# The second-layer matmuls of the last batch put in another order: two runs of narrow matmuls in a quad where there were five

## The chip, the cores and the metric

The kernel runs on 1 core of one Trainium2 chip. The metric is the time of one execution on the device, in microseconds (us), as the median of several runs. The core has five engines that run their own instruction streams: TensorE (PE) multiplies matrices, and its weight loads are shown apart (PEld); VectorE (DVE) and ScalarE (ACT) do elementwise work; GpSimd (POOL) here mostly starts one kind of DMA; SyncE (SP) starts the other DMAs. Each engine takes its instructions in the order in which the program lists them, and waits on semaphores for the others.

## The reference, cut to what matters

```python
# B, N, C = 4, 6080, 256; d_ff = 2048
qn = q / (norm(q, axis=1) + 1e-06); kn = k / (norm(k, axis=1) + 1e-06)
s = kn.transpose(0, 2, 1) @ qn / tau        # C x C for each batch
a = softmax(s, axis=-1)
x = (v @ a).reshape(B * N, C)
h = x @ w_in                                # C -> d_ff
g = h - tanh(h)
out = g @ w_out                             # d_ff -> C
```

Every token's 256 features are mixed by the batch's attention matrix, widened to 2048, passed through h - tanh(h) and brought back to 256.

## The kernel before, in words

**First layer.** For each batch the attention matrix is folded into `w_in` once, so that h is one product of v with a folded factor. The tokens of a batch are cut into 6 pairs of two blocks of up to 512 columns (the odd pair is 512 + 448), and d_ff into 8 slices; a `Quad` (L1138 on) is one pair with one slice: 2 x 2 blocks of 128 factor columns by 512 tokens. It is computed with 7 block products instead of 8 (p1 to p7, `product`, L1329), and each block product is three matmuls, because both operands are kept as an upper and a lower piece (L327, `products`: upper by lower, upper by upper, lower by upper). The sums stand in banks called x, y and z, and ScalarE copies x out (L1173) before the next product is added to it.

**The elements between.** Each of the four blocks 11, 12, 21 and 22 of a quad is made by a DVE addition (L1183), a tanh on ScalarE (L1300, L1195, L1207) and a subtraction; then ScalarE rounds it to its upper piece (`gh`, L1311) and DVE takes the lower piece (`gl`, L1315). In the last batch the subtraction of some blocks (11 and 12) is done by an adding DMA that POOL starts (`join`, L1198 and L1303): the tanh is negated and the DMA adds the block to it.

**Second layer.** Plain blocks (L1470, `second`) take 6 matmuls of 512 columns each: three into each of the two output halves m = 0 and m = 1. They are called ps_o. In pairs 1 to 5 of the last batch ("halved" pairs, 40 quads) the first column of the quad, blocks 11 and 21, is again computed with 7 products instead of 8, at half the width: 21 narrow matmuls of 256 columns (L1393, `second_halves`, ps_h), three for each product. Their inputs come as four items: b1 (one product), b2, t1 and t2 (two products each), made by `split` (L1216) from the tiles n, b and ts. The second column, items 22 and 12, stays plain: 12 matmuls of 512 columns. So a halved quad has 21 matmuls of the first layer and 12 + 21 of the second.

**What sets the order.** The program adds operations to a `Plan` in the order in which TensorE is to run them. Items that are ready for the second layer are appended to a list, `stream`; between the block products of the first layer the table `HALVES` says how much of it `drain` takes (a wide matmul counts 1, a narrow one 0.5; 22.5 for a quad), and `lag` is how far the second layer is held behind. The other engines' operations are then sorted by the plan by when TensorE needs them. So the order of `stream` sets where narrow and wide matmuls stand, and the plan moves ACT's and DVE's work after it. At the very end `stream.sort` puts the plain items of the last `LAST` quads behind everything else.

**A pair's ends.** The last quad of a pair completes the output; the two halves m = 0 and 1 of a column are copied out by DVE and ScalarE (L1493) and stored (L1496), and the first quad of the next pair writes the same banks again. For a halved pair the seven sums ps_h are joined by `gather_halves`: two ScalarE copies (L1417), then DVE additions (L1422, L1435 to L1437) and two stores (L1425).

Of the kernel before, what the change touches and what calls it, by code (L numbers as in the profile page):

```python
# [43 lines left out]
]  # L44
HALVES = [("p6",[]),("p2",[5.5,"c"]),("p5",[]),("p7",[5.0]),("p4",["d",2.5]),("p3",["a",4]),("p1",["b",5.5])]
HALF = NMAX // 2
LAST = 2
SHARE = 1
JOINED = [(),(11,12)]
PARTS = [(1,"start"),(2,"start"),(3,"start"),(4,"start")]  # L50
LATE = {(1,12):3.5,(2,11):2,(2,12):1.5}
SUMS_AT = 32
ENTER = 10
EARLY = 6
# [194 lines left out]
def act_cost(n):  # L249
    return 0.09 + n * 0.00084  # L250
# [15 lines left out]
def attn_moe(ctx: ExitStack, tc: tile.TileContext, qk, v4, qkT, tau, w_in, w_out, outT):  # L266
# [7 lines left out]
    B, N, _, C = qk.shape  # L274
# [853 lines left out]
    def halved(b, p):  # L1128

        return b == B - 1 and p > 0  # L1130
# [7 lines left out]
    class Quad:  # L1138
# [77 lines left out]
        def split(self, name, n, source, reads, place):  # L1216

            x = self.g[name] = {}
            if place is None:
                h, l = Buf(ring["gh"]), Buf(ring["gl"])  # L1220
            else:
                h = Buf(ring[place])
                l = Buf(f"{name}_{self.name}", h)

            def hi():
                if place is None:
                    x[0] = sb(g_p, "gh", [P, NMAX], F32R, f"gh{name}_{self.name}")[:, 0:n]
                else:
                    y = sb(qk_p, place, [P, GJ, 2, C], F32R, f"{name}_{self.name}").rearrange("p a x c -> p a (x c)")
                    x[0], x[1] = y[:, 0, 0:n], y[:, 1, 0:n]  # L1230
                nc.scalar.copy(x[0], source())

            def lo():
                if place is None:
                    x[1] = sb(g_p, "gl", [P, NMAX], F32R, f"gl{name}_{self.name}")[:, 0:n]
                nc.vector.tensor_sub(x[1], source(), x[0].bitcast(F32))

            plan.add("ACT", act_cost(n), hi, reads=reads, writes=[h])
            plan.add("DVE", dve_cost(n), lo, reads=[*reads, h], writes=[l])
            self.bufs["g", name] = h, l  # L1240
            stream.append((self, name))

        def sums(self, i):

# [44 lines left out]
        def finish(self, i, c):  # L1289

            if halved(self.b, self.p) and i % 10 == 1:
                return self.first_column(i)
            n, name = self.ns[i % 10 - 1], f"{i}_{self.name}"
            apart = self.joined(i)
            t, h, l = Buf(ring["t"]), Buf(ring["gh"]), Buf(ring["gl"])
            self.bufs["g", i] = h, l

            def tanh():
                self.tiles["t", i] = sb(g_p, "t", [P, NMAX], F32, f"t{name}")[:, 0:n]
                nc.scalar.activation(self.tiles["t", i], self.tiles[c][:, 0:n], AF.Tanh, scale=-1.0 if apart else 1.0)  # L1300

            def join():
                nc.gpsimd.dma_start(self.tiles["t", i], self.tiles[c][:, 0:n], accum_op=ALU.add)  # L1303

            def sub():
                x = self.tiles["t", i]
                nc.vector.tensor_sub(x, self.tiles[c][:, 0:n], x)  # L1307

            def hi():
                self.g[i] = [sb(g_p, "gh", [P, NMAX], F32R, f"gh{name}")[:, 0:n]]  # L1310
                nc.scalar.copy(self.g[i][0], self.tiles["t", i])  # L1311

            def lo():
                self.g[i].append(sb(g_p, "gl", [P, NMAX], F32R, f"gl{name}")[:, 0:n])
                nc.vector.tensor_sub(self.g[i][1], self.tiles["t", i], self.g[i][0].bitcast(F32))  # L1315

            plan.add("ACT", act_cost(n), tanh, reads=[self.bufs[c]], writes=[t])
            if apart:
                plan.add("POOL", 1.0, join, reads=[self.bufs[c]], writes=[t], port=False, lag=plan.JOIN_LAG + LATE.get((self.s, i), 0.0))
            else:  # L1320
                plan.add("DVE", dve_cost(n), sub, reads=[self.bufs[c]], writes=[t], port=not isinstance(c, str))
            plan.add("ACT", act_cost(n), hi, reads=[t], writes=[h])
            plan.add("DVE", dve_cost(n), lo, reads=[t, h], writes=[l])
            stream.append((self, i))

        def joined(self, i):
            return self.b == B - 1 and i in JOINED[halved(self.b, self.p)]
# [31 lines left out]
        return x.rearrange("p i n -> p (i n)")  # L1359

    stream = []
    outs = {}
    obufs = {}

# [79 lines left out]
    def second(quad, i):  # L1444

        if isinstance(i, str):
            yield from second_halves(quad, i)
            return
        b, p, s = quad.b, quad.p, quad.s
        row, c = i // 10 - 1, i % 10 - 1  # L1450
        n = quad.ns[c]
        f = 2 * s + row
        gh, gl = quad.bufs["g", i]
        key = b, p, c
        first = key not in obufs
        if first:
            obufs[key] = [0] + [Buf(3 + 2 * c + m) for m in range(KC)]
        done = obufs[key]
        done[0] += 1
        last = done[0] == 2 * NS2  # L1460

        parts = (0, 1, 0, 0), (0, 0, 0, 1), (1, 1, 0, 0), (1, 0, 0, 1), (1, 0, 1, 2), (0, 0, 1, 2)
        end = last and b == B - 1 and p == NP - 1
        if end:
            parts = parts[0:2] + parts[5:6] + parts[2:5]
        for m, part, x, j in parts:
            def run(m=m, part=part, x=x, j=j):
                if first and j == 0:
                    outs[key + (m,)] = bank(3 + 2 * c + m, f"ps_o_{b}_{p}_{c}_{m}")
                nc.tensor.matmul(  # L1470
                    outs[key + (m,)][:, 0:n], (wo_l if part else wo_h)[:, f, m * P:(m + 1) * P], quad.g[i][x],
                    start=first and j == 0, stop=last and j == 2, skip_group_check=True,
                )

            plan.add("PE", pe_cost(n), run, reads=[gl if x else gh, wobuf[s]], writes=[done[1 + m]])
            yield 1
        if last:
            at_ = b * N + pairs_of[b][p][0] + c * quad.ns[0]
            for m in range(KC):
                halves = b == B - 1  # L1480
                ob = Buf(ring[("t" if halves else "raw") if c else "ob"])
                tiles = {}

                def copy(m=m, tiles=tiles):
                    if halves:
                        tag = "t" if c else "ob"
                        tiles[0] = sb(g_p, tag, [P, NMAX], F32, f"ob_{b}_{p}_{c}_{m}")[:, 0:n]
                    elif c:
                        raw = sb(qk_p, "raw", [P, GJ, 2, C], F32, f"ob_{b}_{p}_{c}_{m}")
                        tiles[0] = raw[:, 0].rearrange("p x c -> p (x c)")[:, 0:n]  # L1490
                    else:
                        tiles[0] = sb(g_p, "ob", [P, NMAX], F32, f"ob_{b}_{p}_{c}_{m}")[:, 0:n]
                    (nc.scalar.copy if m else nc.vector.tensor_copy)(tiles[0], outs[key + (m,)][:, 0:n])  # L1493

                def store(m=m, tiles=tiles):
                    nc.sync.dma_start(outT[m * P:(m + 1) * P, at_:at_ + n], tiles[0])  # L1496

                plan.add("ACT" if m else "DVE", act_cost(n) if m else dve_cost(n), copy, reads=[done[1 + m]], writes=[ob])
                plan.add("SP", 0.35, store, reads=[ob], size=0.26, due=plan.pe_time + 8.0)
# [277 lines left out]
    for b in range(1, B):  # L1777
        g0 = (b - 1) * SLOTS
        first = NS2
# [13 lines left out]
    lag = LAG  # L1793
# [19 lines left out]
    for gs in range(TOTAL):  # L1813
        quad = quads.pop(gs)
        for what in beside.get((gs, "start"), ()):
            what()
        before, uneven = uneven, quad.ns[0] != quad.ns[1]
        if halves_from - 4 <= gs < halves_from:
            lag += 3
        if gs == halves_from:  # L1820
            lag += 3
        if before and not uneven:
            lag += ENTER if gs < halves_from else 0
            stream[-2:] = reversed(stream[-2:])
        for name, then in UNEVEN if uneven else HALVES if halved(quad.b, quad.p) else ORDER:
            if uneven and not before and name in ("p2", "p5"):
                drain(ENTER // 2)
            if name == "p1":
                if gs + 1 < TOTAL:
                    quads[gs + 1] = Quad(gs + 1)  # L1830
                    quads[gs + 1].product("p1")
            else:
                quad.product(name)
            for x in then:
                if not isinstance(x, str):
                    held = min(lag, x * SHARE if gs >= halves_from else x)
                    lag, x = lag - held, x - held
                    drain(x)
                else:
                    for what in beside.get((gs, x), ()):  # L1840
                        what()
# [66 lines left out]
```

## Time and profile before

| what | value |
|---|---|
| median of 3 runs | 2142.55 us (2141.93 to 2142.94) |
| the profiled execution: its own time | 2142.2 us |
| the profiled execution: its span, first to last instruction | 2140.4 us |
| PE busy | 2134.6 us (100%), 10026 matmuls |
| DVE busy | 1879.3 us (88%) |
| ACT busy | 1613.0 us (75%) |
| POOL busy | 106.8 us (5%) |
| DMA | 419.74 MB, mean 196 GB/s |

The span lies 1.8 us below the execution's own time; the rest is before the first and after the last instruction. The page names TensorE as the engine of 99% of the chain that ended last. Matmuls overlap in the pipeline: the length of one in a timeline (0.39 us for 512 columns) is longer than the distance to the next one's start, so in what follows matmuls are priced by the distance from start to start.

### The profile page before, as it was taken

The page shows a single profiled execution, that of the slowest core. Times are in us where ns is not written, and L with a number is a line of the kernel's source. Part 1 is how long each engine was busy: PE and PEld are TensorE (multiplying, and loading weights), DVE is VectorE, ACT ScalarE, POOL GpSimd, SP SyncE. Part 2 cuts the span into 40 slices and gives each one's busy share as a digit, 9 for nine tenths or more (in the row PEclk, how much of TensorE's full clock was granted, in tenths as well). Part 3 has the DMA queues.
Part 4 walks back from the last instruction along what each step waited for, and adds up shares of the span by engine and source line. Part 5 has one row for each costly group of instructions (what it writes and reads, how often), then busy time and mean ns, then how long its engine had stood idle before and what let it go on. Part 6 is the DMA issues. An engine that isn't in the chain of part 4 may idle for free.

```text
span 2140.4 us, 29514 instructions
## 1 busy us (share of the span) xinstructions
PE 2134.6 (100%) x10026; PEld 1802.5 (84%) x10026; DVE 1879.3 (88%) x3332; ACT 1613.0 (75%) x3015; POOL 106.8 (5%) x117
## 2 busy tenths in 40 slices
PE   9999999999999999999999999999999999999999
PEld 8888888888888888888888888888888888888888
DVE  8998988899898888888899888888888989899897
ACT  6677878777777787886777788887676777777776
POOL 5100000000000000000000000000000011111111
PEclk9999999999999999999999999999999999999999
DMA  9845675366335576643543567564353467887875
GB/s 388 302 163 196 213 252 215 137 202 214 136 136 190 212 244 212 217 163 108 199 138 126 180 231 242 200 224 161 110 198 121 157 200 212 232 222 212 232 210 138
DMA packets 145625, 419.74 MB, mean 196 GB/s; under 512 B 20866, under 2 KB 63106, under 8 KB 142914
## 3 DMA queue, kind: packets, MB, share of 16 engines
q1 hardware_dynamic: 133954, 396.87, 53.3%
q0 software_dynamic: 11520, 20.98, 5.4%
q8 instruction: 79, 1.29, 0.2%
q14 instruction: 72, 0.59, 0.1%
HBM read 329.19 MB, written 66.85 MB: 185 GB/s over the span
## 4 chain that ended last, share of the span: by engine, by line
PE 99%; DMA 1%; issue 0%; ACT 0%; SPq 0%; POOL 0%; POOLq 0%
PE ps_o L1470 43%; PE x L327 25%; PE y L327 12%; PE z L327 7%; PE ps_h L1393 5%; PE ps_s L327 3%; PE ps_s L654 2%; PE ps_s L652 1%; PE ps_w L327 1%; DMA t<-c 0%; DMA vhl<-qk_dram 0%; ACT ob L1493 0%; ACT gh L1311 0%; POOL n L1198 0%; SPq L594 0%
## 5 line engine op out<-in xcount | busy, mean ns | idle before, releaser
L327 PE MATMUL x<-v,f 128*128 128x512 f32 (+1 forms) x2304 | 628.3, 389 | 0.0
L1470 PE MATMUL ps_o<-gh,wo_l 128*128 128x512 f32 (+1 forms) x1376 | 533.4, 388 | 0.2 <-ACT ob L1493 0.2
L1470 PE MATMUL ps_o<-gh,wo_h 128*128 128x512 f32 (+1 forms) x1376 | 533.3, 388 | 0.0
L327 PEld LDWEIGHTS x<-v,f 128*128 128x128 f32 x2304 | 430.1, 188 | 84.5
L1315 DVE TENSOR_TENSOR gl<-t,gh 128x512 fp32r<-128x512 f32 (+1 forms) x688 | 456.7, 681 | 27.0 <-ACT gh L1311 26.0
L1311 ACT CAST gh<-t 128x512 fp32r<-128x512 f32 (+1 forms) x688 | 411.3, 616 | 35.3 <-DVE t L1307 20.5
L1470 PE MATMUL ps_o<-gl,wo_h 128*128 128x512 f32 (+1 forms) x1376 | 421.3, 387 | 0.0
L1300 ACT ACTIVATE t<-c 128x512 f32<-128x512 f32 x536 | 333.2, 624 | 89.0 <-DVE c L1183 82.8
L1307 DVE TENSOR_TENSOR t<-c,t 128x512 f32<-128x512 f32 (+1 forms) x496 | 334.9, 679 | 25.3 <-ACT t L1300 20.2
L1173 ACT COPY u<-x 128x512 f32<-128x512 f32 (+1 forms) x384 | 222.2, 579 | 166.9 <-PE x L327 164.0
L1183 DVE TENSOR_TENSOR c<-u,y 128x512 f32<-128x512 f32 (+1 forms) x384 | 259.3, 675 | 84.6 <-ACT u L1173 55.9
L327 PE MATMUL y<-v,f 128*128 128x512 f32 (+1 forms) x1152 | 320.4, 386 | 0.1
L1470 PEld LDWEIGHTS ps_o<-gl,wo_h 128*128 128x128 f32 x1376 | 258.4, 188 | 51.3
L1470 PEld LDWEIGHTS ps_o<-gh,wo_l 128*128 128x128 f32 x1376 | 258.4, 188 | 48.0 <-ACT ob L1493 0.6
L1470 PEld LDWEIGHTS ps_o<-gh,wo_h 128*128 128x128 f32 x1376 | 258.6, 188 | 47.5
L327 PEld LDWEIGHTS y<-v,f 128*128 128x128 f32 x1152 | 209.8, 188 | 36.6 <-DVE c L1183 0.5
L1183 DVE TENSOR_TENSOR c<-p,z 128x512 f32<-128x512 f32 x192 | 131.8, 686 | 36.1 <-PE z L327 33.4
L327 PE MATMUL z<-v,f 128*128 128x512 f32 x576 | 162.1, 390 | 0.0
L1300 ACT ACTIVATE t<-x 128x512 f32<-128x512 f32 x152 | 91.1, 599 | 93.2 <-PE x L327 92.5
L1307 DVE TENSOR_TENSOR t<-x,t 128x512 f32<-128x512 f32 x152 | 105.1, 691 | 44.2 <-ACT t L1300 43.5
L327 PEld LDWEIGHTS z<-v,f 128*128 128x128 f32 x576 | 108.1, 188 | 23.1
L1173 ACT COPY p<-x 128x512 f32<-128x512 f32 x192 | 112.9, 588 | 19.0 <-PE x L327 16.0
(215 smaller groups left out, 2193.8 us busy)
## 6 DMA issues: line engine op xcount, KB each, us to landing
f<-f_d SPq DMA_DIRECT2D x160, 896.0 KB, 4.6
raw<-qk_dram SPq DMA_DIRECT2D x104, 384.0 KB, 5.0
nt<-qkT_dram SPq DMA_DIRECT2D x96, 380.0 KB, 5.0
f_d<-f SPq DMA_DIRECT2D x32, 896.0 KB, 3.9
outT_dram<-ob SPq DMA_DIRECT2D x88, 256.0 KB, 3.2
vraw<-v_dram SPq DMA_DIRECT2D x20, 1024.0 KB, 7.8
sl<-so_d SPq DMA_DIRECT2D x40, 512.0 KB, 4.0
wt<-wt_d SPq DMA_DIRECT2D x24, 512.0 KB, 6.8
```

Source lines behind the costliest of these rows:

```text
L327: ins = nc.tensor.matmul(out, w, x, start=first and i == 0, stop=last and i == len(seq) - 1, skip_group_check=True,)
L652: nc.tensor.matmul(self.ps[:, 0:C], x[:, 1, k], x[:, 0, q], start=False, stop=last, skip_group_check=True)
L654: nc.tensor.matmul(self.ps.rearrange("p (a c) -> p a c", a=2), x[:, 0, k], x[:, :, q], start=first, stop=False, skip_group_check=True,)
L1173: nc.scalar.copy(self.tiles[to], self.tiles["X"][:, 0:n])
L1183: nc.vector.tensor_add(self.tiles[i], self.tiles[u], self.tiles[ps][:, 0:n])
L1300: nc.scalar.activation(self.tiles["t", i], self.tiles[c][:, 0:n], AF.Tanh, scale=-1.0 if apart else 1.0)
L1307: nc.vector.tensor_sub(x, self.tiles[c][:, 0:n], x)
L1311: nc.scalar.copy(self.g[i][0], self.tiles["t", i])
L1315: nc.vector.tensor_sub(self.g[i][1], self.tiles["t", i], self.g[i][0].bitcast(F32))
L1393: nc.tensor.matmul(outs[b, p, place][:, at_ * HALF:(at_ + 1) * HALF], weights(a, part), quad.g[name][x][:, half * HALF:(half + 1) * HALF], ...
L1470: nc.tensor.matmul(outs[key + (m,)][:, 0:n], (wo_l if part else wo_h)[:, f, m * P:(m + 1) * P], quad.g[i][x], start=first and j == 0, stop ...
```

## The change

The items of a halved quad no longer enter `stream` as they are made. A new function `enter` holds them until their turn in `SEQ`: 22, b1, b2, t1, t2, 12. `lag` grows by 2 and not by 3 where the halved pairs begin. `LAST` is 1: only the last quad's plain items stand behind everything else. In the first and the last quad of every pair of the last batch the six matmuls of a plain item run as three for output half 0 and then three for half 1; before, that was so for the very last item alone.

```diff
@@ -44,11 +44,12 @@
 ]
 HALVES = [("p6",[]),("p2",[5.5,"c"]),("p5",[]),("p7",[5.0]),("p4",["d",2.5]),("p3",["a",4]),("p1",["b",5.5])]
 HALF = NMAX // 2
-LAST = 2
+LAST = 1
 SHARE = 1
 JOINED = [(),(11,12)]
 PARTS = [(1,"start"),(2,"start"),(3,"start"),(4,"start")]
 LATE = {(1,12):3.5,(2,11):2,(2,12):1.5}
+SEQ = [22,"b1","b2","t1","t2",12]
 SUMS_AT = 32
 ENTER = 10
 EARLY = 6
@@ -1238,7 +1239,7 @@
             plan.add("ACT", act_cost(n), hi, reads=reads, writes=[h])
             plan.add("DVE", dve_cost(n), lo, reads=[*reads, h], writes=[l])
             self.bufs["g", name] = h, l
-            stream.append((self, name))
+            enter(self, name)
 
         def sums(self, i):
 
@@ -1321,7 +1322,7 @@
                 plan.add("DVE", dve_cost(n), sub, reads=[self.bufs[c]], writes=[t], port=not isinstance(c, str))
             plan.add("ACT", act_cost(n), hi, reads=[t], writes=[h])
             plan.add("DVE", dve_cost(n), lo, reads=[t, h], writes=[l])
-            stream.append((self, i))
+            enter(self, i)
 
         def joined(self, i):
             return self.b == B - 1 and i in JOINED[halved(self.b, self.p)]
@@ -1359,6 +1360,17 @@
         return x.rearrange("p i n -> p (i n)")
 
     stream = []
+    waiting = {}
+
+    def enter(quad, name):
+        if not halved(quad.b, quad.p):
+            stream.append((quad, name))
+            return
+        there, order = waiting.setdefault(quad.gs, (set(), list(SEQ)))
+        there.add(name)
+        while order and order[0] in there:
+            stream.append((quad, order.pop(0)))
+
     outs = {}
     obufs = {}
 
@@ -1461,7 +1473,7 @@
 
         parts = (0, 1, 0, 0), (0, 0, 0, 1), (1, 1, 0, 0), (1, 0, 0, 1), (1, 0, 1, 2), (0, 0, 1, 2)
         end = last and b == B - 1 and p == NP - 1
-        if end:
+        if end or b == B - 1 and (first or last):
             parts = parts[0:2] + parts[5:6] + parts[2:5]
         for m, part, x, j in parts:
             def run(m=m, part=part, x=x, j=j):
@@ -1818,7 +1830,7 @@
         if halves_from - 4 <= gs < halves_from:
             lag += 3
         if gs == halves_from:
-            lag += 3
+            lag += 2
         if before and not uneven:
             lag += ENTER if gs < halves_from else 0
             stream[-2:] = reversed(stream[-2:])
```

TensorE, steady state, from the narrow matmuls of quad 1 on to quad 2, pair 2 of the last batch. A name ends in batch, pair, quad, sometimes a bank or half, and a serial number: x, y, z are first-layer sums, gh12 and gl12 the pieces of item 12, glb1 and ghb1 those of b1. Before:

```order
L1393 MATMUL ps_h_3_2_7_19131<-t2_3_2_1_19160,wo_h_95 128x256
L1393 MATMUL ps_h_3_2_7_19131<-t2_3_2_1_19160,wo_l_96 128x256
L1470 MATMUL ps_o_3_2_1_0_19057<-gh12_3_2_1_19205,wo_l_96 128x512
L1470 MATMUL ps_o_3_2_1_0_19057<-gh12_3_2_1_19205,wo_h_95 128x512
L1470 MATMUL ps_o_3_2_1_1_19063<-gh12_3_2_1_19205,wo_l_96 128x512
L1470 MATMUL ps_o_3_2_1_1_19063<-gh12_3_2_1_19205,wo_h_95 128x512
L327 MATMUL x_3_2_3_19190<-v5_3_2_18652,f_163_18964 128x512 x3
L1470 MATMUL ps_o_3_2_1_1_19063<-gl12_3_2_1_19215,wo_h_95 128x512
L1470 MATMUL ps_o_3_2_1_0_19057<-gl12_3_2_1_19215,wo_h_95 128x512
L1393 MATMUL ps_h_3_2_3_19043<-glb1_3_2_2_19241,wo_h_95 128x256
L327 MATMUL y_3_2_3_19246<-v6_3_2_18514,f_163_18964 128x512 x3
L1393 MATMUL ps_h_3_2_3_19043<-ghb1_3_2_2_19228,wo_h_95 128x256
```

Now, from the same product of quad 3 on:

```order
L328 MATMUL x_3_2_3_19189<-v5_3_2_18733,f_163_18966 128x512 x3
L1482 MATMUL ps_o_3_2_1_0_19037<-gl12_3_2_1_19236,wo_h_95 128x512
L1482 MATMUL ps_o_3_2_1_0_19037<-gh22_3_2_2_19205,wo_l_96 128x512
L1482 MATMUL ps_o_3_2_1_0_19037<-gh22_3_2_2_19205,wo_h_95 128x512
L328 MATMUL y_3_2_3_19243<-v6_3_2_18517,f_163_18966 128x512 x3
L1482 MATMUL ps_o_3_2_1_1_19054<-gh22_3_2_2_19205,wo_l_96 128x512
L1482 MATMUL ps_o_3_2_1_1_19054<-gh22_3_2_2_19205,wo_h_95 128x512
L1482 MATMUL ps_o_3_2_1_1_19054<-gl22_3_2_2_19215,wo_h_95 128x512
L1482 MATMUL ps_o_3_2_1_0_19037<-gl22_3_2_2_19215,wo_h_95 128x512
L328 MATMUL x_3_2_4_19302<-v0_3_2_18163,f_164_19095 128x512 x3
L1405 MATMUL ps_h_3_2_3_19070<-glb1_3_2_2_19263,wo_h_95 128x256
L1405 MATMUL ps_h_3_2_3_19070<-ghb1_3_2_2_19252,wo_h_95 128x256
```

The narrow matmuls of t2 and b1, which stood as a run of 2, a run of 1 and a run of 2 between wide ones, have left this place; t2 now ends the run of 11 ahead of it, and b1 heads a run of 10 behind it. The run of 5 grew to 10, and the run of 11 is as long as before.

ScalarE, quad 4 of pair 2 (u3 is the copy of x that the next product waits for, n11 the tanh that a POOL DMA joins). Before:

```order
L1195 ACTIVATE n11_3_2_4_19372<-c11_3_2_4_19348 128x512
L1173 COPY u3_3_2_4_19378<-x_3_2_4_19303 128x512
L1231 CAST t1_3_2_3_19383<-ts_3_2_3_19363 128x512
L1231 CAST t2_3_2_3_19391<-ts_3_2_3_19363 128x512
L1207 ACTIVATE t21_3_2_4_19396<-x_3_2_4_19303 128x512
```

Now:

```order
L1174 COPY u3_3_2_4_19376<-x_3_2_4_19302 128x512
L1232 CAST t1_3_2_3_19381<-ts_3_2_3_19365 128x512
L1232 CAST t2_3_2_3_19389<-ts_3_2_3_19365 128x512
L1208 ACTIVATE t21_3_2_4_19394<-x_3_2_4_19302 128x512
L1196 ACTIVATE n11_3_2_4_19401<-c11_3_2_4_19345 128x512
```

The tanh of block 11 has moved from ahead of u3 to behind the tanh of block 21, four operations later.

TensorE, the last two quads of the program. Before:

```order
L1393 MATMUL ps_h_3_5_7_21988<-t2_3_5_6_22561,wo_h_95 128x256 x2
L1393 MATMUL ps_h_3_5_7_21988<-t2_3_5_6_22561,wo_l_96 128x256
L1393 MATMUL ps_h_3_5_3_21903<-glb1_3_5_7_22629,wo_h_95 128x256
L1393 MATMUL ps_h_3_5_3_21903<-ghb1_3_5_7_22616,wo_h_95 128x256
L1393 MATMUL ps_h_3_5_3_21903<-ghb1_3_5_7_22616,wo_l_96 128x256
L1393 MATMUL ps_h_3_5_3_21903<-b2_3_5_7_22603,wo_h_95 128x256 x2
```

Now:

```order
L1405 MATMUL ps_h_3_5_7_21980<-t2_3_5_6_22578,wo_h_95 128x256 x2
L1405 MATMUL ps_h_3_5_7_21980<-t2_3_5_6_22578,wo_l_96 128x256
L1482 MATMUL ps_o_3_5_1_0_21893<-gh12_3_5_6_22582,wo_l_96 128x512
L1482 MATMUL ps_o_3_5_1_0_21893<-gh12_3_5_6_22582,wo_h_95 128x512
L1482 MATMUL ps_o_3_5_1_1_21912<-gh12_3_5_6_22582,wo_l_96 128x512
L1482 MATMUL ps_o_3_5_1_1_21912<-gh12_3_5_6_22582,wo_h_95 128x512
L1482 MATMUL ps_o_3_5_1_1_21912<-gl12_3_5_6_22592,wo_h_95 128x512
L1482 MATMUL ps_o_3_5_1_0_21893<-gl12_3_5_6_22592,wo_h_95 128x512
L1405 MATMUL ps_h_3_5_3_21927<-glb1_3_5_7_22640,wo_h_95 128x256
L1405 MATMUL ps_h_3_5_3_21927<-ghb1_3_5_7_22632,wo_h_95 128x256
L1405 MATMUL ps_h_3_5_3_21927<-ghb1_3_5_7_22632,wo_l_96 128x256
```

Quad 6's item 12, six wide matmuls, moved from behind the last narrow run to ahead of it. On DVE the order behind the last narrow run is as before: five additions of L1422 and L1435 to L1437, then gl12 of quad 7, two more additions, and the copy of output half 0; only ahead of them have gl22 and the last lower piece of t2 changed places.

## Rows read from the trace of the kernel before

**Rows 1.** Cores and page, part 1: span and granted clock; busy time of TensorE.

```profile
core 0: 2140.4 us, clock 1.000
PE 2134.6 (100%) x10026; PEld 1802.5 (84%) x10026; DVE 1879.3 (88%) x3332; ACT 1613.0 (75%) x3015; POOL 106.8 (5%) x117
```

**Rows 2.** Waits of TensorE, whole span: engine line waited for, us, times, longest.

```profile
PE idle L1851 <- DVE ones L319: 1.1, 1, 1.1
PE ps_s L327 <- DMA vhl<-qk_dram: 0.4, 1, 0.4
PE ps_o L1470 <- ACT ob L1493: 0.2, 1, 0.2
```

**Rows 3.** TensorE timeline, 512-column stretch: start, length, engine, line, operation, count.

```profile
1550.25 0.84 PE L327 MATMUL x<-v,f 128*128 128x512 f32 x3
...
1555.91 0.39 PE L1470 MATMUL ps_o<-gh,wo_h 128*128 128x512 f32 x1
```

**Rows 4.** TensorE timeline, one quad of the last batch.

```profile
1840.66 0.28 PE L1393 MATMUL ps_h<-t,wo_h 128*128 128x256 f32 x1
...
1840.89 0.40 PE L1470 MATMUL ps_o<-gh,wo_l 128*128 128x512 f32 x1
...
1842.96 0.28 PE L1393 MATMUL ps_h<-glb,wo_h 128*128 128x256 f32 x1
1843.07 0.86 PE L327 MATMUL y<-v,f 128*128 128x512 f32 x3
1843.77 0.28 PE L1393 MATMUL ps_h<-ghb,wo_h 128*128 128x256 f32 x1
...
1844.00 0.40 PE L1470 MATMUL ps_o<-gh,wo_l 128*128 128x512 f32 x1
...
1846.05 0.40 PE L1393 MATMUL ps_h<-b,wo_h 128*128 128x256 f32 x2
...
1846.64 0.86 PE L327 MATMUL x<-v,f 128*128 128x512 f32 x3
...
1848.03 0.28 PE L1393 MATMUL ps_h<-b,sl 128*128 128x256 f32 x1
...
1849.34 0.86 PE L327 MATMUL y<-v,f 128*128 128x512 f32 x3
...
1850.73 0.28 PE L1393 MATMUL ps_h<-t,wo_h 128*128 128x256 f32 x1
```

**Rows 5.** TensorE timeline, where the last batch passes to its second pair.

```profile
1727.82 0.39 PE L1470 MATMUL ps_o<-gh,wo_l 128*128 128x512 f32 x1
1728.35 0.96 PE L327 MATMUL y<-v,f 128*128 128x512 f32 x3
```

**Rows 6.** Timeline of all engines, the last microseconds.

```profile
2131.71 0.41 DVE L1422 TENSOR_TENSOR ob<-s,ps_h 128x256 f32<-128x256 f32 x1
...
2133.55 0.68 DVE L1315 TENSOR_TENSOR gl<-t,gh 128x512 fp32r<-128x512 f32 x1
...
2134.60 0.81 SPq L1425 DMA_DIRECT2D outT_dram<-ob  x2
...
2135.34 0.39 PE L1470 MATMUL ps_o<-gl,wo_h 128*128 128x512 f32 x1
...
2136.45 0.59 ACT L1493 COPY ob<-ps_o 128x512 f32<-128x512 f32 x1 [4.24 <-PE ps_o L1470]
2136.49 0.90 SPq L1496 DMA_DIRECT2D outT_dram<-ob  x2
```

**Rows 7.** The tile n, whole span: issue to landing of the DMAs that write it.

```profile
DMA to landing us min/median/max: 3.2/4.1/7.6
```

**Rows 8.** Timeline of all engines, one quad of the last batch.

```profile
1851.01 0.86 POOL L1198 DMA_DIRECT2D n<-c  x1 [4.46 <-ACT n L1195]
...
1852.78 0.60 ACT L1207 ACTIVATE t<-x 128x512 f32<-128x512 f32 x1 [0.22 <-PE x L327]
...
1861.00 0.59 ACT L1173 COPY u<-x 128x512 f32<-128x512 f32 x1
```

## The prediction

> **What bounds the kernel now.** I began with the span and the clock: 2140.4 us at a granted clock of 1.000, so TensorE stood at the upper of its two levels, 2.4 GHz, and it was busy for 2134.6 us [rows 1]. The list of TensorE's waits is next: 1.1, 0.4 and 0.2 us are all that it holds, and only the last of them, on an output copy, is in the last batch [rows 2]. So the kernel is bound by TensorE's own pace. A change of order can win what the order itself costs, and lose whatever wait it creates. DVE at 88% and ACT at 75% matter only where they make TensorE wait.
>
> The order's cost is to be read from start to start. In a stretch with 512-column matmuls only, 25 of them lie between 1550.25 and 1555.91: 0.2264 us each [rows 3]; half of that, 0.113, is what a narrow one would take in proportion. Then one quad of the last batch, from one pair of t matmuls (1840.66) to the next (1850.73): 10.07 us for 33 wide and 21 narrow matmuls [rows 4]. In proportion these are 43.5 x 0.2264 = 9.85 us. So 0.2 us of a quad is the price of mixing, and 40 quads make 9 us. This is the ceiling of what the steady part of the change could return; no order that keeps narrow matmuls would return all of it.
>
> **Steady state, piece by piece** [rows 4]. Piece by piece, what is over the proportion:
> - run of 2 (t): 1840.66 to 1840.89, 0.23, nothing over. The 9 wide after it, to 1842.96: 2.07 against 2.04, 0.03 over.
> - run of 1 (glb): 0.11, nothing. The 3 wide after it, to 1843.77: 0.70 against 0.68, 0.02 over.
> - run of 2 (ghb): 0.23, nothing. The 9 wide after it, to 1846.05: 2.05 against 2.04, 0.01 over.
> - run of 5 (b): 1846.05 to 1846.64, 0.59 against 0.57, 0.02 over. The 6 wide after it, to 1848.03: 1.39 against 1.36, 0.03 over.
> - run of 11: 1848.03 to 1849.34, 1.31 against 1.25, 0.06 over. The 6 wide after it, to 1850.73: 1.39, 0.03 over.
>
> Two costs show. The first narrow matmul of a run is free, and each later one takes 0.119 instead of 0.113 (0.06 over ten). And the wide ones after a run pay 0.03 until they are back in step, as much after 2 narrow ones as after 11. So a run's end has a price, not its length alone. The change removes the ends of three runs, 0.03 + 0.02 + 0.01 = 0.06 us, and puts the five narrow matmuls of these runs into the run of 10, where each pays 0.006: 5 x 0.006 = 0.03 us. The ends of the runs of 10 and 11 have six wide matmuls behind them as now and cost the same. Net **-0.03 us a quad, x 40 = -1.2 us**. The rows are rounded to 0.01 us, so three short ends and five small steps leave 0.015 to 0.045: -0.6 to -1.8 us.
>
> The Trainium skill speaks against this gain (TensorE: Matmul & The Clock Gate, Back-to-back issue gap, and LDWEIGHTS): a warm matmul of 256 columns takes 262 cycles, which at 2.4 GHz is an estimated 109 ns, and a load of 128 weight columns P / 1.2 = 107 ns, so the load would stay just hidden and no place in the order would cost anything. The rows differ: 0.119 us inside a run, 0.113 at its head. By the page the steady term would be zero, which is the first rival below.
>
> **The entry to the halved pairs.** There TensorE starts a y product 0.53 us after a single wide matmul [rows 5]: the y bank is free only when DVE has taken z out of it, so 0.53 - 0.23 = 0.30 us is lost. Now one more wide matmul, of item 12, stands ahead of this y; it fills 0.23 us of the hole: -0.2 us. A little later the wait of 0.2 us for an output copy [rows 2] is on output half 1; ordering half 0 first puts half 1 two matmuls back within its item, but the item itself stands earlier now, since b1's matmuls are no longer ahead of it. From no gain to as much again lost, I take zero. Together **-0.2 us**, bounds -0.4 and +0.3. At the other four passages between pairs the list shows no wait, so half 0 first has nothing to win there.
>
> **The tail.** Six wide matmuls (quad 6's item 12) go from behind the last narrow run to ahead of it, so that run ends 6 x 0.2264 = 1.36 us nearer to the end. The additions of `gather_halves` wait for it, and the last lower piece, gl12 of quad 7, stands behind five of them on DVE, as before. Today the first addition starts at 2131.71 and gl12 at 2133.55; TensorE uses gl12 at 2135.34, 1.1 us after it ended [rows 6]. Shifted by 1.36, gl12 would run from 2134.91 to 2135.59 and TensorE would wait 0.25 and see the piece a little after its end: I take **0.3 us**. The final copy follows by as much (today 2136.45). And the two stores of the halves, issued at 2134.60, come out near 2136.0, at most 0.9 us ahead of the last two (2136.49 today); if their transfers queue, the last store ends later still. I take **+0.4 us** for the tail; bounds 0 (DVE finds a gap in which gl12 goes earlier) and +1.0 (the transfers queue in full).
>
> **Covers that the change thins out.** The tanh of block 11 now stands behind the tanh of block 21 on ScalarE. POOL's joining DMA waits for it, so it goes out not at 1851.01 but after 1852.78 + 0.60 + 0.63, near 1854.0 [rows 8]; ScalarE rounds the joined tile (ghb1) just ahead of the copy u3, which runs at 1861.00 and for which TensorE's next x product waits. That leaves about 6.5 us for a landing of 4.1 median, 7.6 at worst [rows 7]. I cost this at nothing, since the median leaves 2.4 us; if that cover is gone, every us of lateness holds ScalarE, then the x product. DVE and ACT have the same instructions as before, and SP the same DMAs.
>
> **Sum.** Profiled execution 2142.2 (span 2140.4 plus 1.8 around it): -1.2 - 0.2 + 0.4 = -1.0, so 2141.2. The median of the runs shown is 0.35 above the profiled one, so 2142.55 - 1.0 = **2141.6 us**, 0.05% faster. What a measurement here can tell from no change is about 0.2%, 4.3 us: below 2138.3 is faster, above 2146.8 slower.
>
> **Rivals.**
> - *The order is neutral.* The wide matmuls pay the same in other places; for it speaks that the pieces I add up are 0.01 to 0.03 us; against it, that a run's end of 2 costs as much as one of 11. Then -0.2 + 0.4: 2142.8 us. The page's rule above gives this time too.
> - *Each run has one price.* If the 0.2 us were a price for each run, two runs in place of five would return 3/5 of it, 0.12 x 40 = 4.8 us, and with the other terms the time were 2138.0 us: faster. Against it: the run of 11 is 0.06 over inside itself, which a lone matmul isn't.
> - *Slower: the joined tile 11 lands too late.* With f loads and two joins closer together, landings go past 6.5 us. ScalarE then stands at ghb1 with u3 behind it, and TensorE at its x product. It decides from 6.5 us on; a landing at the worst seen, 7.6, costs 1.1 us. If 8 of the 40 quads had it, that is 8.8 us and 2150.4 us; from five such quads on (5.5 - 1.0 = 4.5) the result counts as slower. Against it: a median landing has 2.4 us to spare, and the instructions and DMAs are the same in number.
> - *That it doesn't do what it says* is excluded: the order shows two runs, of 10 and 11, in the steady quads.
>
> **How the numbers follow.** The forecast 0.70; the neutral order 0.14; the tail or the entry at its worse bound, or one or two late joins (2142.5 to 2146), 0.07; late joins in five or more quads 0.06; one price for each run 0.03. Within 0.2% are the first three, 0.91; slower 0.06, faster 0.03. The range goes from 1.4 us below the forecast (steady -1.8, entry -0.4, tail at +0.2 or so), 2140.2, up over the neutral order and the worse tail to 2144.0; outside are the slow and the fast rival and the ends of the bounds, less than 2 in 10.
>
> **What would show it.** Right: a steady quad in 10.04 us instead of 10.07; no excess but behind the runs of 10 and 11, 0.03 each; the narrow matmuls of a run still 0.119 apart; the wait in front of the y product at the entry near 0.1; a start of the last gl12 matmul about 0.3 us late against its neighbours; TensorE's list of waits still under 1 us in the last batch. Wrong: a quad still at 10.07 (neutral), at 9.95 (one price), or ScalarE idle ahead of ghb1 with a DMA named and holes ahead of x products (late joins).

## The result and the profile after

The changed kernel takes 2154.0 us (median of 6 runs, 2152.6 to 2155.9), the kernel before 2142.7 us (6 runs beside them): ratio 1.0054, 95% interval 1.0043 to 1.0064. That is 11.3 us slower, outside the range given. The profiled execution took 2153.4 us.

Cores, busy times, and TensorE's waits in the last batch (engine and line, what it waited for, us, times, longest):

```profile
core 0: 2151.6 us, clock 1.000
PE 2143.2 (100%) x10026; PEld 1800.3 (84%) x10026; DVE 1880.3 (87%) x3332; ACT 1611.3 (75%) x3015; POOL 106.9 (5%) x117
PE x L328 <- ACT u L1174: 1.3, 3, 0.6
PE ps_o L1482 <- DVE ob L1505: 0.8, 3, 0.3
PE y L328 <- DVE c L1184: 0.4, 1, 0.4
PE ps_o L1482 <- ACT ob L1505: 0.2, 1, 0.2
```

Clock and work are those of [rows 1]. TensorE's list of waits is longer than in [rows 2], but holds 2.7 us, not 11: a stall is not told by this list alone. The other engines' lists say where to look; in the kernel before, neither line is there:

```profile
ACT ghb L1232 <- DMA n<-c: 35.6, 17, 3.0
DVE ts L1257 <- DMA n<-c: 23.4, 17, 2.1
```

17 times each, ScalarE and VectorE stood waiting for the joined tile of block 11. First, though, a quad in which nothing waits, TensorE's timeline from one glb matmul to the next:

```profile
1775.13 0.28 PE L1405 MATMUL ps_h<-glb,wo_h 128*128 128x256 f32 x1
...
1777.71 1.11 PE L1405 MATMUL ps_h<-t,sl 128*128 128x256 f32 x8
...
1779.02 0.86 PE L328 MATMUL y<-v,f 128*128 128x512 f32 x3
...
1785.17 0.28 PE L1405 MATMUL ps_h<-glb,wo_h 128*128 128x256 f32 x1
```

The quad takes 10.04 us, where [rows 4] had 10.07, and its run of 11 narrow matmuls 1.31 us (1777.71 to 1779.02), as before. Of the last batch's 37 intervals like this one (the tail's two shorter ones left out), 19 are 10.03 or 10.04 us. The other 18 are longer, by 11.7 us together: this is the whole loss.

A quad that loses, timeline of all engines:

```profile
1853.40 0.60 ACT L1208 ACTIVATE t<-x 128x512 f32<-128x512 f32 x1 [0.24 <-PE x L328]
...
1853.90 0.62 ACT L1196 ACTIVATE n<-c 128x512 f32<-128x512 f32 x1
...
1854.70 0.32 SPq L911 DMA_DIRECT2D f<-f_d  x1
...
1854.88 0.86 POOL L1199 DMA_DIRECT2D n<-c  x1 [7.40 <-DVE n L1212]
...
1861.29 0.41 ACT L1232 CAST ghb<-n 128x256 fp32r<-128x256 f32 x1 [1.43 <-DMA n<-c]
1861.29 0.42 DVE L1257 TENSOR_TENSOR ts<-n 128x256 f32<-128x256 f32 x1 [1.13 <-DMA n<-c]
...
1863.10 0.68 DVE L1184 TENSOR_TENSOR c<-u,y 128x512 f32<-128x512 f32 x1
...
1863.86 0.94 PE L328 MATMUL y<-v,f 128*128 128x512 f32 x3
```

The tanh of block 11 (L1196) stands behind that of block 21 (L1208), as forecast, and the join goes out at 1854.88, 0.18 us behind a load of f. It lands 6.4 us later. What the DMA queues moved in the 4.2 us after its issue, and in the 2.8 us after that (queue, packets, MB, share of the 16 engines):

```profile
q1 hardware_dynamic: 118, 0.85, 80.9%
...
q0 software_dynamic: 273, 0.51, 100.4%
q1 hardware_dynamic: 33, 0.10, 13.1%
```

At first only the load's queue moves; the join's has no packet until nearly all of the load's 0.9 MB is through. In the quiet quad the join goes out at 1772.57, 1.17 us ahead of its f load (1773.74), and lands in 4.1 us. In the changed kernel's order the tanh stands behind that of block 21 in exactly 17 of the 40 quads (quads 4 to 7 of a pair and 0 of the next, from the third pair on), one place ahead of it in most others. In 16 of the 17 an f load goes out 0.15 to 0.52 us ahead of the join, and the join lands in 6.0 to 7.4 us; each of these 16 is waited for. In the seventeenth, quad 5 of the last pair, the f loads are over. Its tanh stands behind as well, but its join lands early and nobody waits for it:

```profile
2116.91 0.86 POOL L1199 DMA_DIRECT2D n<-c  x1 [6.25 <-DVE t L1237]
n<-c POOLq DMA_DIRECT2D x1, 256.0 KB, 3.2
```

The seventeenth wait (2008.56) is in quad 2 of pair 4, whose join goes out 1.17 us ahead of its f load, but with loads of vraw on both sides (1995.44 and 2002.23): it lands in 7.8 us.

**Theory A**: the loss is a meeting of two DMAs. In 16 quads the join is issued just behind an 896 KB load, its packets go after the load's, and what reads the joined tile stands first in the queues of ScalarE and VectorE. **Rival B**: the loss is the new order of TensorE itself (the runs, item 22 ahead of b1, half 0 first). **Rival C**: the later tanh alone, whatever DMA it meets.

### The profile page after: what moved, and what is told of

Read it like the earlier page. It is cut to its first block, busy times and chain, and to the rows that moved or that the text cites. A ratio compares the mean times of both kernels' runs of the same rounds, so it can differ in the third digit from the quotient of the medians.

```text
span 2151.6 us, 29481 instructions
## 1 busy us (share of the span) xinstructions
PE 2143.2 (100%) x10026; PEld 1800.3 (84%) x10026; DVE 1880.3 (87%) x3332; ACT 1611.3 (75%) x3015; POOL 106.9 (5%) x117
## 5 line engine op out<-in xcount | busy, mean ns | idle before, releaser
L1482 PE MATMUL ps_o<-gl,wo_h 128*128 128x512 f32 (+1 forms) x1376 | 429.0, 387 | 0.1
```

The lines of the kernel that those rows point to most:

```text
L1482: nc.tensor.matmul(outs[key + (m,)][:, 0:n], (wo_l if part else wo_h)[:, f, m * P:(m + 1) * P], quad.g[i][x], start=first and j == 0, stop ...
```

## Experiments on the meeting of join and load

In these kernels marked steps change places after the planner is done, so that nothing else moves. `mark["n", gs]`, `mark["t", gs]`, `mark["f", gs]`, `mark["s", gs]` are quad gs's tanh of block 11, tanh of block 21, f load and sl load.

**One place ahead.**

```diff
+        for gs in range(halves_from, TOTAL):
+            if mark["n", gs].start > mark["t", gs].start:
+                mark["n", gs].start = mark["t", gs].start - 1e-6
```

> The changed kernel with one thing altered: in the 17 quads of the last batch in which ScalarE takes the tanh of block 11 behind the tanh of block 21, the two change places (34 rows of ScalarE's order; no other engine's order changes). In the changed kernel's trace the joining DMA of these quads goes out 0.15 to 0.5 us behind an f load and lands after 5.6 to 6.7 us; in the other quads it goes out 1.2 us ahead of the f load and lands after 3.1 to 4 us. Theory A (the joins come late because they queue behind the f load, and ScalarE, waiting for them in order, holds the copies for which TensorE waits): the joins go out ahead of the f loads again and land in 3 to 4 us, the gaps of TensorE in these quads (8.2 us by the trace) go, the median is 2145.8 us, or less if the waits at the starts of the pairs come from the same cause. Rival B (the loss is the new order of the narrow matmuls itself, or the halves' order at the pairs' ends): 2154 us as before the swap, within 1 us. Rival C (the later tanh is late for another reason than the DMA, and half a microsecond earlier only shortens the wait by as much): gaps shorter, 2149 to 2152 us.

Measured: 2150.6 us, ratio 1.0039 (1.0024 to 1.0054). Only 3.4 us came back, the size that rival C gave, but the joins had not become punctual. The first of a stretch:

```profile
1863.81 0.86 POOL L1199 DMA_DIRECT2D n<-c  x1 [4.94 <-ACT n L1196]
1864.46 0.32 SPq L911 DMA_DIRECT2D f<-f_d  x1
n<-c POOLq DMA_DIRECT2D x1, 256.0 KB, 6.5
```

0.65 us ahead of the load is not enough: the landing still takes 6.5 us. Here the packets of both queues move side by side. After the first stalls the lead shrinks, to 0.1 us at the end of the stretch. I had taken the lead of 1.2 us from other quads without working it out for these; that expectation was wrong, and the run leaves A and C both open.

**Two places ahead.**

```diff
-                mark["n", gs].start = mark["t", gs].start - 1e-6
+                mark["n", gs].start = mark["t2", gs - 1].start - 1e-6
```

(`mark["t2", gs - 1]` is the ScalarE cast just ahead.)

> The changed kernel with the tanh of block 11 moved two places ahead on ScalarE in the 17 quads in question (ahead of the second ts cast), where one place gave 2150.6 us: there the joins went out 0.1 to 0.65 us ahead of the f load and still landed in 6.1 to 7.2 us. In all traces so far a join that goes out 1.0 us or more ahead of the f load lands in 3.1 to 3.9 us (when nothing else is in its way), one that goes out 0.65 us ahead or less in 5.6 to 7.2 us. Theory A (which of the two transfers reaches the DMA engines first decides): 0.52 us earlier again makes the lead 1.17 us, as in the first pair's quads; the joins land in 3.1 to 3.9 us and the time is that of the kernel with the f loads put back, 2142.5 to 2143.5 us. Rival C (each half microsecond of ScalarE's order is worth the 3.4 us that the first one brought): 2147 us. Rival D (moving the ts cast behind costs as much as it brings, because TensorE's run of narrow matmuls waits for it): 2146 us and more, with new gaps in the narrow runs.

Measured: 2143.0 us, ratio 0.9999 (0.9990 to 1.0008): all of the loss is gone, and 32 of the 37 intervals are 10.04 us. One of its joins:

```profile
1864.21 0.86 POOL L1199 DMA_DIRECT2D n<-c  x1 [4.36 <-ACT n L1196]
1865.38 0.32 SPq L911 DMA_DIRECT2D f<-f_d  x1
n<-c POOLq DMA_DIRECT2D x1, 256.0 KB, 3.4
```

Two equal steps of 0.5 us on ScalarE brought 3.4 and 7.6 us, and the landing fell from 6.5 to 3.4 us at the second. C, which prices the tanh's time, doesn't explain this; how far the join is ahead of the load does.

**The load later instead**, ScalarE's order left as it is.

```diff
+                f = min(fs, key=lambda op: abs(op.start - n - 3.5))
+                later = [op.start for op in ss if op.start > f.start]
+                if f.start > n and later:
+                    f.start = min(later) + 1e-6
```

(for the 17 quads; `n` is the start of the tanh, `fs` and `ss` are the f and sl loads)

> The changed kernel with ScalarE's order untouched (the tanh of block 11 still behind that of block 21 in 17 quads), but the f loads that go out just ahead of these joins put behind the next sl load in SP's queue, about 5 us later (only SP's order changes). It tells the two halves of theory A apart from each other: if the landing is late because the f load's packets are ahead of the join's on the DMA engines, the joins of these quads land in 3 to 4.5 us although they are issued no earlier, and the time is 2145 to 2147.5 us. If the joins are simply issued too late, the landing stays near what it is or the gaps stay, and the time stays at 2153 to 2155 us. Rival B (narrow order, halves' order): 2154 us. A risk: the f and sl loads back to back may meet the join of the next quad, which would leave part of the loss, 2148 to 2152 us.

Measured: 2142.75 us, ratio 0.9999 (0.9989 to 1.0008). The join goes out as late as in the changed kernel, and its tile is there in time:

```profile
1860.39 0.53 SPq L911 DMA_DIRECT2D f<-f_d  x1
...
1865.18 0.86 POOL L1199 DMA_DIRECT2D n<-c  x1 [5.58 <-ACT n L1196]
...
n<-c POOLq DMA_DIRECT2D x1, 256.0 KB, 3.2
PE ps_o L1483 <- ACT ob L1506: 0.3, 1, 0.3
```

So the late tanh costs nothing by itself. B falls too: TensorE's order is the changed one to the last row, and the loss is gone, the waits at the pairs' starts (0.8 us in the list of the changed kernel) among it: these followed from the late joins.

**The cause put into the kernel before**, whose narrow runs are the old five.

```diff
+        for f in fs:
+            later = [op.start for op in ss if op.start > f.start]
+            if f.start > mark["n", halves_from + 11].start and later:
+                f.start = min(later) + 1e-6
```

> The control: the kernel before, with the f loads put behind the next sl load in SP's queue in the same way, about 5 us later. In the kernel before, the joins of block 11 go out 2 to 3 us ahead of the f load and land in 3.5 to 4 us. Theory A (the later f load only takes away a collision that the changed kernel has): no change, 2142.5 to 2143.2 us. Rival E (later f loads are a gain of their own, of 11 us, and the narrow order's loss is hidden by it): 2132 to 2140 us. Rival F (in this order the later f load meets another join): 2145 to 2155 us.

Measured: 2155.3 us, ratio 1.0059 (1.0045 to 1.0073). I had meant it as a control and expected no change; but in this order a load 5 us later stands just ahead of the next join, which is Rival F:

```profile
1850.60 0.42 SPq L910 DMA_DIRECT2D f<-f_d  x1
...
1851.82 0.86 POOL L1198 DMA_DIRECT2D n<-c  x1 [4.46 <-ACT n L1195]
n<-c POOLq DMA_DIRECT2D x1, 256.0 KB, 6.3
PE y L327 <- DVE c L1183: 7.8, 11, 1.3
```

The same meeting, without any of the change and with TensorE's order of before, costs 12.1 us. It is better evidence than the control would have been.

**The cause doubled**: the 18 quads with the tanh one place ahead get it behind as well.

```diff
+            n, t = mark["n", gs], mark["t", gs]
+            if 0.0 < t.start - n.start < 1.0:
+                n.start = t.start + 1e-6
```

> The changed kernel with the suspected cause doubled: in the 18 further quads in which the tanh of block 11 stands one place ahead of the tanh of block 21 on ScalarE, it is put behind it too (36 rows of ScalarE's order, no other engine's order changes), so 35 of 40 quads have it behind. Theory A (join behind the f load): the joins of these quads go out 0.1 to 0.5 us behind the f load instead of 1.2 us ahead, land after about 6 us, and each quad loses about what the 17 lose now, 8.2 / 17 = 0.48 us: 18 x 0.48 = 8.7, so 2162 to 2163 us. Rival B (the narrow runs or the halves' order): no change, 2154 us. Rival C (half a microsecond of ScalarE order with no DMA in it): at most 18 x 0.1, 2155 to 2156 us.

Measured: 2183.8 us, ratio 1.019. The direction is A's, the size isn't: 29.8 us more, not 8.7. The tile n's landings went to 3.2/6.7/8.9 us (minimum, median, maximum) from 3.2/4.8/7.8, and single stalls of TensorE reached 2.6 us. Its list of waits now leads with u3, and behind three of the stalls the granted clock stood at the lower level, one of them here:

```profile
PE x L328 <- ACT u L1174: 19.5, 18, 2.5
1775.50:1778.90 3.40, 3.40 (x10) 2.62 (x9) 2.39 (x5) 2.98 (x6) 0.87 (x1) 0.50 0.32 49
```

At half the clock, three stretches of 3.4 us are an estimated 5 us of the loss. That in a row of late quads one hands its delay to the next, so that the price is not one per quad, is my reading of the rest; no run here shows it by itself.

## By which road the late tile reaches TensorE

The prediction's rival had the road over ScalarE: u3 behind ghb1, the x product behind u3. I put u3 first, in the changed kernel:

```diff
+            if mark["n", gs].start > mark["t", gs].start and mark["u3", gs + 1].start > mark["b1", gs].start:
+                mark["b1", gs].start = mark["u3", gs + 1].start + 1e-6
```

> The changed kernel with the late joins left as they are, and the copy u3 put ahead of the rounding of the joined tile (ghb1) on ScalarE where it stood behind it in the 17 quads in question; VectorE's glb1 follows ghb1. It tells by which road the late tile reaches TensorE. Theory A1 (ScalarE's order: u3 stands behind ghb1, and TensorE's x product waits for u3): the gaps in front of x products go, 2143.5 to 2145 us. Theory A2 (VectorE's order: the subtractions ts on the joined tile hold the addition c, for which TensorE's y product waits): nothing gained, 2153 to 2155 us. Both roads, as the gaps in front of x and of y products suggest (about half of them each): 2147 to 2151 us.

Measured: 2155.2 us, ratio 1.0059 (1.0045 to 1.0072): nothing gained. In the last batch VectorE's list leads with the joined tile, and u3, which headed TensorE's in the changed kernel (1.3 us), has gone from it; the wait for c has grown from 0.4 us (the profiled execution took 2158.5 us, 3.3 more than the median):

```profile
DVE ts L1257 <- DMA n<-c: 24.1, 17, 4.0
PE y L328 <- DVE c L1184: 3.2, 3, 1.9
```

The 24.1 us answer to 23.4 us in the changed kernel. So the road over ScalarE was there, and it was closed, but what it cost came over VectorE. The late quad above shows this second road: ts at 1861.29 on VectorE, in all five subtractions on the late tile (four of ts, one of glb), then c at 1863.10, done at 1863.78, and the y product at 1863.86. In the changed kernel both are open: by the starts of its matmuls, 21 of TensorE's 45 stalls in the last batch stand ahead of x products (3.7 us, of which seven stalls that wait for u3 make 2.4), and 19 ahead of y products (some 2.5 us, most of it for c). Then c ahead of ts as well:

```diff
+                row = [mark["ts", 0, gs], mark["ts", 1, gs], mark["l", "b1", gs], mark["ts", 2, gs], mark["ts", 3, gs]]
+                c = mark["c", 22, gs + 1]
+                for i, op in enumerate(row):
+                    if op.start < c.start:
+                        op.start = c.start + 1e-6 * (i + 1)
```

> The changed kernel with the late joins left as they are, and in the 17 quads in question both engines relieved: on ScalarE u3 ahead of ghb1, as in the run before, and on VectorE the addition c (u3 plus y) ahead of the subtractions ts and glb1 that read the joined tile. With u3 alone ahead the time did not fall (2155.2 us), and VectorE still stood 24.1 us ahead of ts. Theory A2 (the late tile reaches TensorE through VectorE: c stands behind ts, and the y product behind c): the gaps in front of y products go; the x product that waits for the subtraction n of block 21, which stands behind the pieces of ts, may keep its gap: 2147 to 2150 us. If c was the only road: 2143 to 2145 us. Rival (the narrow runs wait for the pieces of ts themselves, whatever stands behind them): no gain, 2153 to 2156 us, with gaps inside the narrow runs.

Measured: 2171.9 us, ratio 1.0134 (1.0118 to 1.0150), worse than every case written down. TensorE's waits and VectorE's first:

```profile
PE x L328 <- DVE n L1212: 14.7, 14, 1.1
PE ps_o L1483 <- ACT ob L1506: 5.9, 4, 1.8
PE y L328 <- DVE c L1184: 0.2, 1, 0.2
DVE c L1184 <- ACT u L1174: 38.1, 33, 2.6
```

The y products hardly wait any more, so c behind ts was their road. But VectorE now stands for u3 instead, ts starts later still, and the subtraction n of block 21, behind ts, holds the x products. The joined tile is on no engine's list of waits any more: what is paid here is the new order on VectorE itself. So a late tile reaches TensorE over both engines; in the two orders tried the loss moved to another wait, and in the second it grew.

## The other parts of the change

**Half 0 first undone** at the ends of the pairs:

```diff
-        if end or b == B - 1 and (first or last):
+        if end:
```

> The changed kernel without its last part: at the ends of the last batch's pairs the output halves stand in the old order again (the very end keeps its own). The planner then puts the tanh of block 11 ahead of that of block 21 in all quads by itself, so this is to be compared with the kernel in which the 17 tanhs are swapped back. Theory P (half 0 first causes the four waits of 0.42 us for an output copy on VectorE at the pairs' starts, with the 0.11 us lost behind each): these waits go, and with on-time joins the time is 2143 to 2144 us. Rival Q (item 22 standing ahead of b1 causes them, and half 0 first only makes them shorter): without it TensorE waits about 1 us or more at each of the four starts, 2147 to 2151 us, or, if the late joins stay, 2154 us and more.

Measured: 2148.1 us, ratio 1.0024 (1.0014 to 1.0034), with the joins of nearly all quads punctual. TensorE's waits:

```profile
PE ps_o L1482 <- DVE ob L1505: 3.9, 5, 0.8
PE y L328 <- DVE c L1184: 1.0, 1, 1.0
```

At each of five pairs' starts TensorE loses 0.9 to 0.95 us and 0.11 behind it. Rival Q's case came: the waits come from the rest of the change, and half 0 first takes four of the five away (with punctual joins only the first is left, 0.5 to 0.9 us), some 4 us. That it is item 22 ahead of b1 that makes them, and not the smaller `lag`, is argued from the order; no run here separates the two. The rest of the 5 us to the 2143.0 and 2142.75 us above is about the one wait for c in the list.

**The tail undone**, on top of the later loads:

```diff
-LAST = 1
+LAST = 2
```

> The kernel with the f loads put behind the sl loads (2142.75 us), and in addition only one thing of the change undone: at the very end the items 12 of the last two quads stand last again, not of the last one alone. It prices the tail. Prediction's step: the tail costs 0.3 to 0.4 us as changed, and the trace shows 0.25 us of wait and 0.11 behind it at the last lower piece; undone, the time is 2142.3 to 2142.4 us, which only the trace can tell from 2142.75. Rival: the two stores that come out earlier or later decide, 2142.0 or 2143.2 us. Against the kernel before: the steady quads return 1.2 us, and the entry and single gaps elsewhere cost about 1.2 us: 2142.0 to 2142.8 us, no difference that can be measured.

Measured: 2143.45 us, ratio 1.0001 (0.9992 to 1.0010); no difference to 2142.75 that these runs can tell. The trace has no stall at gl12 any more, and the span ends 4.4 us after the last matmul starts, as before, where the changed tail has 4.75; but there are 1.3 us of gaps in the last narrow runs. I expected the changed tail to be the dearer one; by the trace it is the cheaper, by the times neither.

**Half 0 first undone at the first two pairs' starts only**, on top of the tanh two places ahead:

```diff
-        if end or b == B - 1 and (first or last):
+        if end or b == B - 1 and (first and p > 1 or last):
```

> The candidate: the changed kernel with the tanh of block 11 two places ahead (2143.0 us), and half 0 first undone at the starts of the last batch's first two pairs alone, where the trace shows an output copy waited for 0.77 us and 0.11 lost behind it (0.35 and 0.18 in the kernel before). If half 0 first made that wait longer, 0.3 to 0.4 us come back: 2142.6 us, and 0.6 us (0.03%) less than the kernel before, less than a measurement can tell. If the wait comes from item 22 standing ahead of b1, it stays or grows to 1.1 us, as at the starts of the later pairs without half 0 first: 2143.0 to 2143.6 us.

Measured: 2143.0 us, ratio 0.9998 (0.9989 to 1.0007). The wait at the entry stayed (`PE ps_o L1483 <- ACT ob L1506`, 0.7 us). No kernel here is measurably faster than the one before.

## Why the prediction was wrong, point by point

- **What bounds the kernel**: right, TensorE's pace, with any wait to be paid.
- **Steady state, -0.03 us a quad**: right. 10.04 us wherever nothing waits, and narrow matmuls 0.119 us apart inside a run; the gain is as small as said. One piece of its sum is too large: it counts five narrow matmuls that pay 0.006 us more, but the second one of a run of 2 was 0.119 us long before, too, so three do. The estimate from the Trainium skill (TensorE: Matmul & The Clock Gate, Back-to-back issue gap and LDWEIGHTS) had no gain at all; the trace doesn't agree.
- **Entry, -0.2 us**: right for the y product, whose wait fell from 0.30 to 0.08 us (1728.36 to 1728.67); the output copy is waited for as long as before (0.63 us from start to start, 0.58 before).
- **Half 0 first has nothing to win**: the step looked at the order before, in which b1 stands between the pair's last output and item 22. In the new order it saves some 4 us.
- **Tail, +0.4 us**: the wait for gl12 came as worked out (0.25 us, and 0.11 behind it). In addition the span ends 4.75 us after the last matmul starts, 4.4 before, in line with the stores queuing, as the upper bound allowed. Together 0.7 us, within the bounds.
- **"I cost this at nothing, since the median leaves 2.4 us"**: this step failed. It took the landing of 4.1, at worst 7.6 us [rows 7] as a draw from a lot that moving the join doesn't touch, and so put the wait for the joined tile at nothing. Measured, 16 of the moved joins landed in 6.0 to 7.4 us; with either the join or the load moved out of the other's way, all of the 11 us came back. A landing hangs on what is issued around it, and the trace of before showed this twice. The worst one:

```profile
1827.02 0.38 SPq L910 DMA_DIRECT2D f<-f_d  x1
1827.45 0.45 SPq L928 DMA_DIRECT2D vraw<-v_dram  x1
1829.27 0.32 SPq L495 DMA_DIRECT2D sl<-so_d  x1
1830.22 0.86 POOL L1198 DMA_DIRECT2D n<-c  x1 [2.46 <-ACT n L1195]
n<-c POOLq DMA_DIRECT2D x1, 256.0 KB, 7.6
```

and the place for which the prediction moved the join to "near 1854.0":

```profile
1854.03 0.32 SPq L910 DMA_DIRECT2D f<-f_d  x1
```

  The step looked at SP's DMAs, which are the same, and not at their times. With this row the 6 in 100 for late joins should have been the likeliest case.
- **The rival itself** gave 8 quads at 1.1 us, 8.8 us; it was 16 quads with some 0.6 us each (the 11.7 us less 1.65 at three pairs' starts and 0.64 for one late join of tile 12, by 16). Its sum was near by luck. Its road (ScalarE, u3) is one of two; it left out the one over VectorE.

Without the meeting the profiled kernel with the tanh two places ahead has a span of 2141.3 us, 0.9 above [rows 1]; but TensorE reaches the entry 0.9 us later already (1728.92 with one matmul more done, against 1727.82 in [rows 5]), so the last batch takes about what it took: its 37 intervals are 1.3 us shorter together, the tail is 0.7 us longer, and the wait for the output copy at the entry 0.4 us. The runs put it 0.2 us below the kernel before, the prediction 1.0 us. Whether the new order itself is worth 1 us, these runs can't tell.

## What to carry to other kernels

When a change moves the issue of a DMA, don't take its landing from a median: put the new issue time beside every other queue's issues, and let a large transfer that goes out within 1.2 us ahead of it, or 0.65 us behind it, count in full. An engine's list of waits for a DMA that the kernel before doesn't have finds such a loss at once, though TensorE's own list holds a quarter of it. And before a narrow order is blamed, put the suspected meeting into the old kernel: here it cost about the same there.

## What the runs showed of the hardware

- A POOL-issued join 0.18 us behind a 896 KB SP load had no packet in 4.2 us; 0.65 us ahead of it, the packets of the two moved side by side and it landed in 6.5 us; in the changed kernel 1.0 to 1.2 us ahead of it, 3.4 to 5.2 us, and 7.8 us in the one quad above; with no load near, 3.2 us. The Trainium skill (DMA: Bandwidth & Descriptors, Queues, rings and completion order) says that the DMA engines take turns between queues packet by packet. The second case agrees. The first doesn't show it: there nearly the whole load went first. Whether the join's part was already with the DMA engines in that time, the trace doesn't tell.
- A stall of TensorE mostly costs more than its length: the matmul that was held takes 0.11 us longer to the next one's start (1743.50 to 1743.83, 0.33 instead of 0.23 us). By the starts of its matmuls the changed kernel has 45 stalls of over 0.05 us in the last batch, 8.1 us by themselves, and behind 32 of them 3.5 us in what follows; the kernel before has 3. The list of waits shows 2.7 us of it.
- Behind a stall of 2.0 us (c ahead of ts, from 1911.5) the granted clock fell to the lower level for some 3.4 us; the stall of 1.3 us at 1900.8 left it where it was. But another stall of 2.0 us in the same kernel, up to 2093.8, left it there too, and with the cause doubled so did one of 2.6 us, up to 1834.7; these runs show no length from which it falls. The stretches (us, busy times and counts, granted clock, DMA share, GB/s), the last one behind the stall up to 2093.8:

```profile
1900.00:1911.00 11.00, 9.90 (x54) 8.29 (x53) 8.68 (x17) 6.91 (x14) 1.72 (x2) 1.00 0.75 210
1915.20:1918.40 3.20, 3.20 (x14) 3.00 (x13) 3.08 (x7) 1.35 (x3) 0.00 (x0) 0.51 1.03 357
2094.50:2098.00 3.50, 3.50 (x21) 2.97 (x20) 3.50 (x9) 2.04 (x4) 0.00 (x0) 1.00 1.03 320
```
